# Top-k attention and two expert mixtures on one core: where the work ahead of a branch ends

## Chip, cores and metric

One core of a Trainium2 chip runs the whole program in one launch. The metric is the device time of an execution in microseconds (us). The engines are TensorE (PE; its weight loads are PEld), VectorE (DVE), ScalarE (ACT), GpSimd (POOL) and SyncE (SP, which here only issues transfers).

## The reference

```python
def _attn_ref(q, k, v):                      # (2, 8, 576, 64): batch, heads, tokens, width
    scores = q @ k.T / 8                     # per batch and head
    keep the 32 largest of each row, softmax over them, times v
    ...
def _moe_ref(x, domain_probs, w1, w2):       # x 1152 x 512; 4 experts, w1 512 x 1024, w2 1024 x 512
    out += p[:, e:e + 1] * (np.maximum(x @ w1[e], 0.0) @ w2[e])      # every token, every expert
    ...
def _moe2_ref(x, w_gate, w1, w2, capacity):  # 8 experts, capacity 288
    expert_idx = np.argmax(x @ w_gate, axis=1)
    # each token goes to its one expert, at most 288 of them, in order of tokens
    out[i] = gate_w[i] * y[expert_idx[i], pos[i]]
```

How many tokens an expert of the second mixture has is known only on the chip.

## The kernel before

**Order.** The program is written engine by engine by a planner that runs while the kernel is built (class `Order`). Each kind of work is a stream, a Python generator (`w_loads`, `w_splits`, `m1`, `hid`, `htr`, `m2`, `outs`, `gathers`, `prep_x` and others), that yields its next step: the engines that could do it with their costs, the events it waits for, and the buffers (`Slots`) it takes. `run` picks the step with the smallest key: its planned start plus the bias of its stream. For a step on TensorE the key is at least the time when the step is ready plus a slack by stream. `self.now` is the planned start of the last step picked, `busy` the planned end of each engine's last step. Where a step has two engines, the second must win by the penalty `pen`, 1.0 us in the stage of the change. The planned times decide the order alone: on the chip each engine runs its own list in order, and waits for semaphores of the others.

**Weights.** A quarter of an expert is a pair of tiles of 128 x 1024 (part 0 for the first product, part 1 for the second), 512 KB each. `w_loads` issues a load on SP (L341) into one of nine raw tiles. `w_splits` makes a high part in the reduced format on ScalarE (L353) and the low part, raw minus high, on GpSimd or VectorE (L355), which frees the raw tile. There are seven high and seven low tiles for each part: four quarters of the running expert, and three of the next. Products are three matrix multiplications (high x high, high x low, low x high).

**The second mixture.** Tokens are routed, and expert `e` has up to three units of 128 tokens (`b` = 0, 1, 2). A unit is: gather its rows of x (POOL, L1071), transpose them (`prep_x`, PE L1083, ACT L1087, DVE L1090), first product per quarter (`m1`, PE L697), ReLU (ACT L719), transpose (`htr`, PE L755), hidden tile's high and low part (ACT L762, DVE L765), second product (`m2`, PE L794), scaled output (ACT L1102), scatter (POOL, L1106). Unit 0 is always run. Units 1 and 2 stand in the bodies of branches (`more`, L1142) on the count of tokens, which is loaded at L1163 on every engine. Within a body only the unit's own streams run: `more` sets the other streams aside and restores the plan behind the body, whether it will run or not. The next expert's unit 0 comes behind the branch. The planner counts a body as taking no time.

Ahead of the branch the loop runs the planner until a list of things has been placed:

```python
        nxt = []
        if e + 1 < E2:
            nxt += [("w", NQ1 + 4 * e + 4 + i, part) for i in range(NXTQ) for part in range(2)]
            nxt += [("xgl", e + 1, 0)] if AHEAD else []
        nxt += [("xgl", e, 1), ("xg", e, 2)]
        o.run(until=lambda: all(x in ev for x in nxt))
```

`("w", j, part)` is a quarter's split, `("xgl", e, b)` the transposed input of a unit, `("xg", e, 2)` a gather. The running expert's four quarters are freed behind the branch.

Of the kernel before, what the change touches and what calls it, by code (L numbers as in the profile page):

```python
# [11 lines left out]
AF = mybir.ActivationFunctionType  # L12
# [18 lines left out]
COLD = 12  # L31
BIAS2 = {"w_splits": 0.5}
AHEAD = 1
BATCH = 4
DRATE = 290e3
SLACK = {"transposes": 1.0, "avs": 0.6, "routes": 2.0, "m1": 0.3, "m2": 0.3, "qks": 0.2}
NXTQ = 3
INF = float("inf")
BELOW = 2.0 ** 80
# [27 lines left out]
class Order:  # L67
# [25 lines left out]
    def run(self, until=None):  # L93
        while self.streams and (until is None or not until()):
            pick = None
            for s in self.streams:
                engs, deps, slots = s[2]
                r = 0.0
                for d in deps:
                    r = max(r, s[4] if d == "<" else self.ev.get(d, INF))  # L100
                if r == INF:
                    continue
                for q in set(slots):
                    r = max(r, sorted(q.free)[slots.count(q) - 1] if slots.count(q) <= len(q.free) else INF)
                if r == INF:
                    continue
                opt = None
                for e, c in engs:
                    c *= 2 if e == "PE" and self.now < COLD else 1
                    st = max(r, self.busy.get(e, 0.0))  # L110
                    pen = 0.0 if opt is None else self.pen
                    if opt is None or st + c + pen < opt[0]:
                        opt = (st + c + pen, st, e, c)
                key = opt[1] + s[0]
                if opt[2] == "PE":
                    key = max(key, r + SLACK.get(s[3], 0.0) + s[0])
                if pick is None or key < pick[0]:
                    pick = (key, s, opt)
            if pick is None:
                raise RuntimeError("no stream can go on: " + str([(s[3], s[2][1]) for s in self.streams]))  # L120
            _, s, (_, st, e, c) = pick
            got = []
            for q in s[2][2]:
                i = q.best()[1]
                q.free[i] = INF
                got.append(i)
            self.now = st
            self.busy[e] = st + c
            s[4] = st + c + self.LAT
            self.step(s, (st + c, e, got))  # L130

    pen = 0.0
    bias = {}

    def rebias(self, bias):
# [4 lines left out]
    def set(self, name, t, lat=None):  # L140
        self.ev[name] = t + (self.LAT if lat is None else lat)
# [10 lines left out]
def c_act(n, ps=False, extra=0):  # L152
    return (n / 1.2 + (55 if ps else 95) + 93 * extra) / 1000


def c_dve(n):
    return (n + 64) / 960
# [11 lines left out]
def kernel(  # L169
# [14 lines left out]
    nc = tc.nc  # L184
# [6 lines left out]
    E2 = moe2_w1.shape[0]  # L191
# [25 lines left out]
    o = Order()  # L217
    ev = o.ev
# [4 lines left out]
    def slots(pool, n, shape, dt, name):  # L223
        return Slots(tiles(pool, n, shape, dt, name))
# [6 lines left out]
    def act(c, deps=(), sl=()):  # L231
        return [("ACT", c)], deps, sl
# [7 lines left out]
    def sub(n, deps=(), sl=()):  # L240
        return [("POOL", c_pool(n)), ("DVE", c_dve(n))], deps, sl

    def eng_of(e):
        return {"POOL": nc.gpsimd, "DVE": nc.vector}[e]
# [71 lines left out]
    NQ1 = len(GROUPS) * E1 * 4  # L316
# [4 lines left out]
    w_lo = [slots(wp, 3, WSH[i], F32R, f"w{i}l") for i in range(2)]  # L321
    w_hi = [slots(wp, 3, WSH[i], F32R, f"w{i}h") for i in range(2)]
# [24 lines left out]
    def w_splits():  # L347
        for j in range(NQF, NQ):
            for part in range(2):
                t, _, (i, l) = yield act(c_act(1024), [("wr", j, part)], [w_hi[part], w_lo[part]])  # L350
                raw, r = W[j, part]
                hi, lo = w_hi[part].tiles[i], w_lo[part].tiles[l]
                nc.scalar.activation(hi, raw, AF.Copy)  # L353
                t, e, _ = yield sub(1024, ["<"])
                eng_of(e).tensor_sub(lo, raw, hi.bitcast(F32))  # L355
                w_raw.free[r] = t
                W[j, part] = [lo, l, hi, i]
                o.set(("w", j, part), t)

    def w_free(j, part, t):  # L360
        if j < NQF:
            w_raw.free[W.pop((j, part))[1]] = t
            return
        _, l, _, h = W.pop((j, part))
        w_lo[part].free[l] = t
        w_hi[part].free[h] = t
# [484 lines left out]
    def logits(tl):  # L851
        n = len(tl)
        t0 = tl[0]
        _, _, (pl_i,) = yield pe(0.01, [("acc", t0)], [banks])
        pl = banks.tiles[pl_i]
        xts = []
        for t in tl:
            _, _, (g, xi) = yield pe(4 * 0.112, [("acc", t)], [banks, xt_s])
            xts.append(xi)
            a = acc_s.tiles[acc[t]]  # L860
            px, xt = banks.tiles[g], xt_s.tiles[xi]
            nc.sync.dma_start(x1[t * P:(t + 1) * P, :], a)
            for c in range(ND):
                nc.tensor.transpose(px[:, c * P:(c + 1) * P], a[:, c * P:(c + 1) * P], ident)
            tm, e, _ = yield [("ACT", c_act(512, True)), ("DVE", c_dve(512))], ["<"], []
            if e == "ACT":
                nc.scalar.activation(xt, px, AF.Copy)
            else:
                nc.vector.tensor_copy(xt, px)
            banks.free[g] = tm  # L870
            acc_s.free[acc[t]] = tm + 3.0
            o.set(("xt", t), tm)
        for i, t in enumerate(tl):
            xt = xt_s.tiles[xts[i]]
            tm, _, _ = yield pe(0.35, [("xt", t)])
            for c in range(ND):
                nc.tensor.matmul(pl[:, i * E2:(i + 1) * E2], xt[:, c, :], wg[:, c, :],
                                 start=(c == 0), stop=(c == ND - 1))
            xt_s.free[xts[i]] = tm
            o.set(("lg", t), tm)  # L880
        if tl[-1] == NT - 1:
            return pl_i
        tm, _, _ = yield dve(0.12, [("lg", tl[-1])])
        nc.vector.tensor_copy(LG[:, t0:t0 + n].rearrange("p n e -> p (n e)"), pl[:, :n * E2])
        banks.free[pl_i] = tm
        for t in tl:
            o.set(("lg", t), tm)
# [121 lines left out]
    def routes():  # L1009
# [3 lines left out]
        early = range(GROUPS[-1][0])  # L1013
        for i in range(0, len(early), BATCH):
            yield from route(early[i:i + BATCH], late_pool[0])
        pl_i = yield from logits(GROUPS[-1])
# [98 lines left out]
    def unit(e, b):  # L1115
        class Lazy:
            def __init__(self, n):
                self.n = n

            def __getitem__(self, key):  # L1120
                return XG[e, b][self.n][key]
        J = Job(("u", e, b), Lazy(0), Lazy(1), 1, [NQ1 + e * 4 + i for i in range(4)], [("xg_ok", e, b)],
                unit_out(e, b), False, True)
        return [o.add(m1([J]), "m1"), o.add(hid([J]), "hid"), o.add(htr([J]), "htr"),
                o.add(m2([J]), "m2"), o.add(outs([J]), "outs")]

    def finish(ss):
        o.run(until=lambda: not any(s in o.streams for s in ss))

    order = [(e, b) for e in range(E2) for b in range(UB)]  # L1130
    ph_s.extend(range(2), o.now)
    o.rebias(BIAS2)
# [6 lines left out]
    def more(e, b):  # L1139
        if b == UB:  # L1140
            return
        with tc.If(n > b * P):  # L1142
            st = o.save()
            o.streams = []
            ss = []
            if b > 1:
                ss.append(o.add(prep_x([(e, b)]), "prep_x"))
            ss += unit(e, b)
            finish(ss)
            more(e, b + 1)  # L1150
            o.restore(st)

    for e in range(E2):
        ev["go", e] = o.busy["PE"]
        finish(unit(e, 0))
        nxt = []
        if e + 1 < E2:
            nxt += [("w", NQ1 + 4 * e + 4 + i, part) for i in range(NXTQ) for part in range(2)]
            nxt += [("xgl", e + 1, 0)] if AHEAD else []
        nxt += [("xgl", e, 1), ("xg", e, 2)]  # L1160
        o.run(until=lambda: all(x in ev for x in nxt))
        o.run(until=lambda: "gates" in ev)
        n = nc.values_load(cnt[0:1, e:e + 1], min_val=0, max_val=NTOK)  # L1163
        more(e, 1)
        XG_s.free[XG[e, 1][2]] = o.busy["PE"]
        for b in range(2, UB):
            xg_s.free[xgs[e, b]] = o.busy["PE"]
        for i in range(4):
            for part in range(2):
                w_free(NQ1 + 4 * e + i, part, o.busy["PE"])  # L1170
# [35 lines left out]
```

## Time and profile before

| what | value |
|---|---|
| three runs, median | 849.49 us (848.1 to 850.31) |
| the profiled execution | 851.02 us, of which 849.0 us are the span from first to last instruction |
| TensorE busy | 777.7 us, 92% of the span |
| VectorE, ScalarE, GpSimd busy | 630.4, 592.2, 419.5 us |
| mean granted TensorE clock | 0.969 of full |
| second mixture | from about 656 us to the end; twelve units (L1106 has 12 scatters) |

By the trace the units of experts 0 to 7 are 2, 1, 2, 3, 1, 1, 1 and 1. In the rows below times are us from the span's start; a row of time order is start, length, engine, line, operation, output<-inputs, count, and in brackets the idle time before it with what ended it.

### The profile page before, as it was taken

The numbers are of one execution on the slowest core, as the hardware profiler recorded it, in microseconds if no ns is written. First come the engines' busy times: TensorE is split into PE (matmuls) and PEld (weight loads), VectorE is DVE, ScalarE is ACT, GpSimd is POOL, SyncE is SP. The second block draws the span as 40 slices with busy tenths as digits, with TensorE's granted clock in tenths as the row PEclk, the third lists the DMA queues.
The fourth block names the chain that finished last, engine by engine and source line by source line (L and its number), as shares of the span: only waits on it lengthen the run. The fifth ranks groups of instructions, "written<-read, shape, count | busy, mean of one in ns | idle before, by whom it ended". The sixth has DMA issues, their size and how long they took to land. (4 is left out here: it accounts for less than half of the span.)

```text
span 849.0 us, 15682 instructions
## 1 busy us (share of the span) xinstructions
PE 777.7 (92%) x5538; PEld 685.4 (81%) x5538; DVE 630.4 (74%) x1475; ACT 592.2 (70%) x1199; POOL 419.5 (49%) x292
## 2 busy tenths in 40 slices
PE   6668999899999999999999999999995989997676
PEld 5557777699889989899988898998983979887665
DVE  6799999999999998999998386568445266515551
ACT  6767878888999988989888765445442356626552
POOL 4332233766779977789985612222333143403321
PEclk9999999899999999999999999999996999999889
DMA  5344865722345543335552698555566159617630
GB/s 139 112 119 118 248 204 184 227 98 96 92 132 170 159 141 119 125 122 177 174 159 85 216 367 286 180 173 171 182 195 207 42 192 311 209 63 223 215 107 10
DMA packets 116953, 138.96 MB, mean 164 GB/s; under 512 B 18911, under 2 KB 84959, under 8 KB 116864
## 3 DMA queue, kind: packets, MB, share of 16 engines
q1 hardware_dynamic: 113712, 129.23, 47.7%
q0 software_dynamic: 2880, 8.52, 3.2%
q8 instruction: 51, 0.84, 0.4%
q14 instruction: 38, 0.31, 0.1%
q10 hardware_dynamic: 272, 0.07, 0.0%
HBM read 130.84 MB, written 7.86 MB: 163 GB/s over the span
## 5 line engine op out<-in xcount | busy, mean ns | idle before, releaser
L554 DVE MAX8 m<-wk 128x8 f32<-128x576 f32 x216 | 158.6, 749 | 0.8
L572 POOL TENSOR_TENSOR e<-sc,e 128x576 f32<-128x576 f32 x72 | 102.5, 1426 | 74.6 <-ACT e L570 66.7
L355 POOL TENSOR_TENSOR w0l<-wraw,w0h 128x1024 fp32r<-128x1024 f32 x42 | 101.3, 2411 | 27.7 <-ACT w0h L353 21.7
L550 DVE MATCH_REPLACE8 wk<-m,wk 128x576 f32<-128x576 f32 x144 | 106.9, 743 | 0.0
L355 POOL TENSOR_TENSOR w1l<-wraw,w1h 128x1024 fp32r<-128x1024 f32 x39 | 93.9, 2408 | 18.8 <-ACT w1h L353 17.9
L737 ACT ACTIVATE hh<-bank 128x256 fp32r<-128x256 f32 x128 | 49.8, 390 | 75.8 <-PE bank L794 65.1
L794 PE MATMUL bank<-w1h,hh 128*128 128x512 f32 x220 | 91.3, 415 | 1.0 <-ACT hh L762 1.0
L794 PE MATMUL bank<-w1h,hl 128*128 128x512 f32 x220 | 86.5, 393 | 0.1
L794 PE MATMUL bank<-w1l,hh 128*128 128x512 f32 x220 | 86.5, 393 | 0.0
L740 DVE SCALAR_TENSOR_TENSOR hl<-bank,hh 128x256 fp32r<-128x256 f32 x128 | 53.6, 420 | 42.3 <-ACT hh L737 41.5
L700 PE MATMUL bank<-xh,w0h 128*128 128x256 f32 x392 | 66.6, 293 | 0.0
L605 PE MATMUL bank<-ident,e 128*128 128x128 f32 x288 | 47.5, 291 | 20.6 <-ACT e L593 20.6
L520 PE MATMUL bank<-kT,qT 128*128 128x288 f32 x320 | 64.2, 333 | 0.7 <-ACT qT L498 0.6
L700 PE MATMUL bank<-xh,w0l 128*128 128x256 f32 x392 | 63.2, 284 | 0.0
L700 PE MATMUL bank<-xl,w0h 128*128 128x256 f32 x392 | 63.0, 283 | 0.0
L581 ACT ACTIVATE e<-e,m 128x576 f32<-128x576 f32 x72 | 56.3, 781 | 9.3 <-POOL e L572 8.6
L570 ACT ACTIVATE e<-sc,m 128x576 f32<-128x576 f32 x72 | 56.3, 783 | 7.3 <-DVE m L557 6.9
L605 PEld LDWEIGHTS bank<-ident,e 128*128 128x128 f32 x288 | 36.0, 148 | 30.8 <-ACT e L593 22.7
L700 PEld LDWEIGHTS bank<-xh,w0h 128*128 128x128 f32 x392 | 55.7, 191 | 4.0 <-issue 1.4
L593 ACT ACTIVATE e<-e,sm 128x576 f32<-128x576 f32 x72 | 56.0, 782 | 4.0 <-DVE sm L590 3.9
L520 PEld LDWEIGHTS bank<-kT,qT 128*128 128x128 f32 x320 | 51.1, 206 | 8.0 <-issue 4.8
L353 ACT ACTIVATE w1h<-wraw 128x1024 fp32r<-128x1024 f32 x52 | 55.8, 1072 | 1.7 <-PE bank L794 1.7
(199 smaller groups left out, 2070.1 us busy)
## 6 DMA issues: line engine op xcount, KB each, us to landing
wraw<-in_moe_w_dram SPq DMA_DIRECT2D x160, 512.0 KB, 3.8
wrawb<-in_moe_w_dram SPq DMA_DIRECT2D x64, 512.0 KB, 4.7
out_dram<-zero SPq DMA_DIRECT2D x9, 256.0 KB, 3.6
x<-acc SPq DMA_DIRECT2D x9, 256.0 KB, 4.2
kr<-in_k_dram SPq DMA_DIRECT2D x8, 256.0 KB, 2.7
vt<-in_v_dram SPq DMA_DIRECT2D x8, 256.0 KB, 3.5
qr<-in_q_dram SPq DMA_DIRECT2D x31, 64.0 KB, 2.3
acc<-x,gidx POOLq DMA_INDIRECT x24, 4.5
```

What stands on the lines that cost most here:

```text
L353: nc.scalar.activation(hi, raw, AF.Copy)
L355: eng_of(e).tensor_sub(lo, raw, hi.bitcast(F32))
L520: nc.tensor.matmul(banks.tiles[g[y]][:, :HS], qT_s.tiles[i][:, 2 * a + m % 2], kT_s.tiles[kT[b, 2 * pr + a]][:, half * HS:(half + 1) * HS] ...
L550: nc.vector.match_replace(wk, m[:, 8 * r - 8:8 * r], s if r == 1 else wk, -3.0e38)
L554: nc.vector.max(m[:, 8 * r:8 * r + 8], wk)
L570: nc.scalar.activation(e, s, AF.Relu, bias=m[:, TOPK:TOPK + 1], scale=-BELOW)
L572: nc.gpsimd.tensor_sub(e, s, e)
L581: nc.scalar.activation(e, e, AF.Exp, bias=m[:, TOPK + 1:TOPK + 2], accum_out=sm_s[a].tiles[i][:, 0:1])
L593: nc.scalar.activation(e, e, AF.Copy, scale=s[:, 1:2])
L605: nc.tensor.transpose(x[:, n * P:(n + 1) * P], p[:, a, a * REST + n * P:a * REST + (n + 1) * P], ident)
L700: nc.tensor.matmul(ph[:, :N], w[:, c, fc * P:(fc + 1) * P], xx[:, c, :N], start=(c == 0 and m == 0), stop=(c == ND - 1 and m == 2))
L794: nc.tensor.matmul(y, hx[:, col:col + P], w[:, fc, :], start=(first and m == 0), stop=(qi == 3 and fc == 1 and m == 2))
```

## The change

Four things change, all in the planner.

- The work ahead of a branch must include only the first quarter of the next expert (both parts), the transposed input of this expert's second unit, and the gather for the third. The rest of the former list is still run for only until a picked step starts later than 0.8 us (`MEET`) ahead of the planned end of TensorE's unit.
- Then `push("w_loads")` runs the loads alone until no raw tile is left to give out.
- In the second mixture's quarters (`j >= NQ1`) the high part may go to ScalarE or VectorE.
- In the second mixture `w_splits` is in `late`: its key, too, is at least the ready time plus a slack, of 0.6 us.

```diff
+MEET = 0.8
...
-SLACK = {"transposes": 1.0, "avs": 0.6, "routes": 2.0, "m1": 0.3, "m2": 0.3, "qks": 0.2}
+SLACK = {"transposes": 1.0, "avs": 0.6, "routes": 2.0, "m1": 0.3, "m2": 0.3, "qks": 0.2, "w_splits": 0.6}
...
                 key = opt[1] + s[0]
-                if opt[2] == "PE":
+                if opt[2] == "PE" or s[3] in self.late:
                     key = max(key, r + SLACK.get(s[3], 0.0) + s[0])
...
+    def push(self, name):
+        kept = self.streams
+        self.streams = [s for s in kept if s[3] == name]
+        gone = list(self.streams)
+        try:
+            self.run()
+        except RuntimeError:
+            pass
+        self.streams = [s for s in kept if s not in gone or s in self.streams]
...
+    late = ()
...
-                t, _, (i, l) = yield act(c_act(1024), [("wr", j, part)], [w_hi[part], w_lo[part]])
+                who = [("ACT", c_act(1024))] + [("DVE", c_dve(1024))] * (j >= NQ1)
+                t, e, (i, l) = yield who, [("wr", j, part)], [w_hi[part], w_lo[part]]
                 raw, r = W[j, part]
                 hi, lo = w_hi[part].tiles[i], w_lo[part].tiles[l]
-                nc.scalar.activation(hi, raw, AF.Copy)
+                if e == "ACT":
+                    nc.scalar.activation(hi, raw, AF.Copy)
+                else:
+                    nc.vector.tensor_copy(hi, raw)
...
+    o.late = ("w_splits",)
...
-        nxt += [("xgl", e, 1), ("xg", e, 2)]
-        o.run(until=lambda: all(x in ev for x in nxt))
+        must = [("xgl", e, 1), ("xg", e, 2)] + nxt[:2 if e + 1 < E2 else 0]
+        end = o.busy["PE"] - MEET
+        o.run(until=lambda: all(x in ev for x in must) and (o.now > end or all(x in ev for x in nxt)))
+        o.push("w_loads")
         o.run(until=lambda: "gates" in ev)
```

## Rows read from the trace of the kernel before

**Rows 1.** The page: TensorE's busy time; the granted clock by slices.
```profile
PE 777.7 (92%) x5538; PEld 685.4 (81%) x5538; DVE 630.4 (74%) x1475; ACT 592.2 (70%) x1199; POOL 419.5 (49%) x292
...
PEclk9999999899999999999999999999996999999889
```

**Rows 2.** Stages: length, busy PE, PEld, DVE, ACT, POOL (x instructions), clock, DMA, GB/s.
```profile
684.00:700.00 16.00, 13.54 (x91) 12.12 (x92) 12.58 (x13) 12.12 (x20) 9.01 (x6) 1.00 0.75 250
700.00:726.00 26.00, 25.22 (x168) 22.65 (x166) 14.22 (x17) 15.44 (x28) 7.49 (x6) 1.00 0.78 257
...
765.00:782.60 17.60, 13.34 (x91) 11.88 (x89) 12.29 (x14) 12.61 (x20) 7.27 (x6) 1.00 0.74 226
782.60:804.40 21.80, 15.20 (x89) 13.40 (x89) 11.99 (x13) 12.07 (x19) 7.57 (x6) 0.83 0.63 208
804.40:827.00 22.60, 16.62 (x88) 14.19 (x89) 11.39 (x13) 12.19 (x19) 4.82 (x3) 0.80 0.40 135
827.00:849.00 22.00, 15.27 (x84) 12.89 (x84) 3.80 (x6) 6.03 (x12) 3.42 (x2) 0.89 0.03 10
```

**Rows 3.** TensorE in order of time: what follows the branches of experts 1 to 6.
```profile
699.73 0.63 PE L1083 MATMUL bank<-ident,acc 128*128 128x128 f32 x4 [2.11 <-DVEq L1142]
...
712.84 0.65 PE L697 MATMUL bank<-w0h,xh 128*128 128x256 f32 x4
...
726.04 0.66 PE L1083 MATMUL bank<-ident,acc 128*128 128x128 f32 x4 [0.82 <-ACTq L1142]
...
782.59 0.71 PE L697 MATMUL bank<-w0hb,xh 128*128 128x256 f32 x4 [4.26 <-DVEq L1142]
...
804.38 1.19 PE L697 MATMUL bank<-w0h,xh 128*128 128x256 f32 x4 [6.53 <-DVEq L1142]
...
827.02 1.19 PE L697 MATMUL bank<-w0hb,xh 128*128 128x256 f32 x4 [5.43 <-DVEq L1142]
```

**Rows 4.** VectorE in order of time: low parts ahead of branches 1, 2, 4, 6.
```profile
696.76 2.82 DVE L355 TENSOR_TENSOR w1lb<-wraw,w1hb 128x1024 fp32r<-128x1024 f32 x1 [0.51 <-ACT w1hb L353]
...
712.11 2.67 DVE L355 TENSOR_TENSOR w1lb<-wraw,w1hb 128x1024 fp32r<-128x1024 f32 x1 [0.67 <-ACT w1hb L353]
...
780.03 1.23 DVE L355 TENSOR_TENSOR w0lb<-wrawb,w0hb 128x1024 fp32r<-128x1024 f32 x1 [1.43 <-ACT w0hb L353]
781.17 1.22 DVE L355 TENSOR_TENSOR w1lb<-wrawb,w1hb 128x1024 fp32r<-128x1024 f32 x1
...
825.60 1.22 DVE L355 TENSOR_TENSOR w1lb<-wrawb,w1hb 128x1024 fp32r<-128x1024 f32 x1
```

**Rows 5.** ScalarE in order of time: high parts (L353) and scaled outputs (L1102).
```profile
695.68 1.04 ACT L353 ACTIVATE w1hb<-wraw 128x1024 fp32r<-128x1024 f32 x1
...
725.26 0.69 ACT L1102 ACTIVATE x1T<-bank,gate 128x512 f32<-128x512 f32 x1 [4.50 <-PE bank L794]
...
778.37 0.69 ACT L1102 ACTIVATE x1T<-bank,gate 128x512 f32<-128x512 f32 x1 [1.21 <-PE bank L794]
778.95 1.05 ACT L353 ACTIVATE w0hb<-wrawb 128x1024 fp32r<-128x1024 f32 x1
779.90 1.04 ACT L353 ACTIVATE w1hb<-wrawb 128x1024 fp32r<-128x1024 f32 x1
...
801.31 1.04 ACT L353 ACTIVATE w1hb<-wrawb 128x1024 fp32r<-128x1024 f32 x1
...
824.13 1.05 ACT L353 ACTIVATE w1hb<-wrawb 128x1024 fp32r<-128x1024 f32 x1
```

**Rows 6.** TensorE in order of time: two first-product quarters; expert 7's input transposed.
```profile
765.13 0.63 PE L697 MATMUL bank<-w0h,xh 128*128 128x256 f32 x4
...
766.91 0.72 PE L697 MATMUL bank<-w0h,xh 128*128 128x256 f32 x4
...
815.75 0.60 PE L1083 MATMUL bank<-ident,acc 128*128 128x128 f32 x4
```

**Rows 7.** SP in order of time: raw loads issued around expert 3's second and third units.
```profile
741.59 27.03 SPq L341 DMA_DIRECT2D wraw<-in_moe_w_dram  x2
```

## The prediction, made before the changed kernel was run

> **What bounds the kernel now.** The page comes first. TensorE is busy 92% of the span, and its granted clock is full in all but the first slices and the last ones [rows 1]. Up to about 640 us nothing the change touches can therefore bring much; what is to be had lies where that row falls, in the second mixture.
>
> The second view is the table by stages, cut at the experts' first units [rows 2]. Of the twelve units that ran, experts 0 and 2 have two, expert 3 has three, and 1, 4, 5, 6 and 7 have one. An expert with one unit costs TensorE 13.3 us (684 to 700: 13.54 busy, 765 to 782.6: 13.34). But the stretches of experts 4, 5 and 6 last 17.6, 21.8 and 22.6 us, and in the last two the clock is 0.83 and 0.80. ScalarE is busy 12.1 to 12.6 us in each, VectorE 11.4 to 12.3. No engine is full, so something makes them take turns.
>
> TensorE's order of time shows what [rows 3]. It stands still 2.10 us before 699.73, 4.26 before 782.59, 6.53 before 804.38 and 5.43 before 827.02, 18.3 us in all, each time released by VectorE's passing of the branch (L1142). These are the branches of experts 1, 4, 5 and 6, whose second unit does not run. At expert 2's branch, where it does run, TensorE goes on at 712.84 with no idle time. After a second unit it waits 0.82 us for ScalarE.
>
> VectorE's and ScalarE's orders of time say what is late [rows 4, 5]. VectorE's last low part ahead of expert 1's branch ends at 696.76 + 2.82 = 699.58, expert 4's at 781.17 + 1.22 = 782.39, expert 6's at 825.60 + 1.22 = 826.82; TensorE starts 0.15 to 0.20 us later in all of the four. So its first matmul of the next expert waits until VectorE has worked off everything that the program put ahead of the branch. Much of that was begun after TensorE had finished: its unit of expert 4 ended at 782.59 - 4.26 = 778.33, and two high parts start on ScalarE at 778.95 and 779.90, behind the scaled output of 778.37; expert 5 has four such (the last at 801.31), expert 6 three (the last at 824.13), nine together. They belong to the second and third quarter of the next expert, which TensorE needs only some microseconds into its next unit. That is the bound: three quarters are demanded ahead of the branch, and the branch makes TensorE wait for them.
>
> **The change, part by part.** *Where the work ahead of the branch ends.* What remains ahead of it is what the planner starts before TensorE's unit ends, the next first quarter, and the second unit's input. ScalarE's scaled output is still there: 0.69 us from 725.26, ended 0.09 before TensorE's 726.04 [rows 3, 5]. So 0.83 us is the floor of a gap. The ceiling is a low part begun just at the unit's end: with 1.23 us plus the 0.20 it gives 1.43. I take 1.1, nearer to the floor because ScalarE's output comes first in any case: four gaps of 18.3 us become 4.4. Gain 13.9 (12.6 to 15.0).
>
> *The clock.* The gap of 2.10 us left the clock at 1.00 (700 to 726); those of 4.26, 6.53 and 5.43 are followed by stretches at 0.83, 0.80 and 0.89, between the levels of 1.2 and 2.4 GHz [rows 2]. TensorE's busy time in these is 15.20, 16.62 and 15.27 us for 89, 88 and 84 matmuls, against 13.34 for 91: 1.9 + 3.3 + 1.9 = 7.1 us more. Gaps of 1.1 us are shorter than the one that did no harm, so I take 6 back (0 if the gaps stay over 4 us).
>
> *The nine high parts and their low parts* move behind the branch, into the next unit, and here is the cost. From a high part's start to its low part's end is 778.95 to 780.03 + 1.23 = 781.26, that is 2.93 us behind the unit's end; two low parts follow each other by 1.14, so a quarter (two splits) takes 2.3 us. TensorE takes its first-product quarters 766.91 - 765.13 = 1.78 apart, a transposing group between them included [rows 6]. With the one guaranteed quarter in hand, TensorE starts 0.83 behind the unit's end and wants the second quarter at 2.6, gets it at 2.9 (wait 0.3); wants the third at 4.7, gets it at 5.2 (0.5); the fourth at 7.0, gets it at 7.5 (0.5). That is 1.3 us in a unit; with two quarters in hand nothing. Expert 4's branch has two done already (only two high parts start behind its unit's end), so expert 5 pays nothing; experts 6 and 7 pay 1.3 each, 2.6. The same two engines must also serve the unit's own hidden tiles, which go first; for that I double it, to 5 us. Bounds: nothing (12.1 us of ScalarE in 14 us leave room), and nine splits with no cover at VectorE's pace, 9 x 1.14 = 10.3.
>
> *The slack of 0.6 us* lets a split be placed behind another engine step due within that time. It can leave VectorE or ScalarE idle up to 0.6 per split, 4.8 for an expert's eight; nothing if the step it yields to releases TensorE. It is held inside the bounds just given, as both engines have about 2 us to spare per unit.
>
> *High parts on VectorE.* The choice costs a microsecond of penalty, so it is taken only where ScalarE's planned queue is over a microsecond behind. The trace has no such copy; the nearest row is the subtraction of the same size, 1.23 us [rows 4], against about 0.95 between high parts on ScalarE [rows 5]. Few will move, VectorE carries as much as ScalarE, and I put it at nothing (plus or minus 1 us for four of them). The Trainium skill (VectorE: DVE Perf Modes, The perf-mode tier table) has a single-source fp32 copy at twice the rate of a two-source operation, 1227 ns for 2048 elements; halved, that would be some 0.6 us as an estimate and would make four of them worth 2 us less VectorE time, the path being the same. No run here shows it.
>
> *Raw loads given out.* SP has only these loads in this stage, so nothing is queued behind them. The merged row at 741.59 [rows 7] stretches over 27.03 us for two issues: one load stood until expert 3's third unit was over. Given out ahead it lands sooner, but no split in the second mixture is shown waiting for a load, so this is worth nothing, in either direction, unless the splits run ahead of the loads.
>
> *The next expert's input* is no longer demanded ahead of the branch. Its transposes stand well within the unit (815.75 for expert 7, while expert 6's unit ends at 827.02 - 5.43 = 821.59 [rows 3, 6]). If they slipped behind the branch, each would cost its 0.6 us of transposes and about the 0.83 floor again, 1.4, 4.2 for three. I take nothing.
>
> Sum: -13.9 - 6 + 5 = -14.9 us. The profiled execution took 851.02 us (span 849.00), 1.53 above the median; it would take 836.1, and the median 849.49 becomes **834.6**. With every term at its good end (-15.0 - 7.1) it is 827.4; at its bad end (-12.6 - 6 + 10.3) 841.
>
> **A rule that speaks against it.** At the four branches TensorE starts within 0.20 us of the end of VectorE's last low part, and at 712.84 it enters a body with no gap [rows 3, 4]. The Trainium skill (Runtime: NRT & Kernel Launch, Instruction fetch mechanics) says that a taken branch whose target lies outside the fetched pages stalls until the target's page has come. By that rule the gaps would belong to the branch, moving work would not shorten them, and the sum would be nothing in place of -14.9; the rows agree with it badly.
>
> **The rivals.**
>
> *Everything is covered.* The two engines' 12 us per expert fit into 14; then no split is waited for: 827 to 828. Against it: each unit's own tiles cut into the splitting.
>
> *The wait moves into the units.* Splits and unit share two queues in program order. If the four units 4 to 7 stay paced by the splits, 15 of the 19.9 us come back as short waits in the middle of the units, and the clock alone is won: 844.5. For it: ScalarE makes the hidden tiles of the unit between the splits, and each of those waits for TensorE, so a split behind one starts late even where its load has long landed. Against it: in expert 1 all eight high parts were done (the last from 695.68) before the unit's end at 697.63 [rows 3, 5].
>
> *The gap is the branch's own.* If jumping over a body that does not run is what costs the 2.1 to 6.5 us, on whichever engine, the four gaps of 18.3 us and the slow clock behind them stay: 849.5. For it: the long gaps come only where a second unit's body is jumped over. Against it: the 0.15 to 0.20 us behind VectorE's last low part at all four, and the 0.82 us behind expert 2's second unit, where the third unit's body is jumped over too [rows 3, 4].
>
> *Slower: the stock shrinks.* A quarter not split before a second unit isn't split during it either. The units of experts 2 to 7 would then start with one quarter instead of three. It decides at 19.9 / 6 = 3.3 us of waiting per unit, which is where TensorE takes the quarters one by one (a quarter 2.3 us late twice); at 4 us per unit the time is 849.5 + 24 - 19.9 = 853.6. Against it: expert 1 again; in experts 1 to 3 little is left to defer.
>
> **How the numbers follow.** Forecast (829 to 841) 0.50; everything covered 0.14; wait moves into the units 0.18; branch's own 0.08; slower 0.10. Range 826 to 846: it holds the first three, 0.82. A change under 0.3% (2.5 us) can't be told from none by a measurement of this kernel. Faster by more: 0.82; within: 0.08; slower: 0.10.
>
> **What would show it.** Right: the idle time before the first matmul of experts 2, 5, 6 and 7 is 0.8 to 1.5 us, released by ScalarE or VectorE at the branch; clock about 1.00 from 765 on; new waits for low parts (L355 or its successor) inside the units of experts 6 and 7, 5 us together; stretches of experts 4, 5 and 6 of 14 to 16 us. Wrong: gaps unchanged though VectorE is through earlier; waits over 3 us in each first unit; TensorE waiting at units' starts for an input transposed behind the branch; splits waiting for raw loads.

## The result, and the profile after

The changed kernel takes 841.74 us (five runs, 840.96 to 842.24), the kernel before 849.82 (five runs, 848.1 to 850.63): a ratio of 0.9901 with a 95% interval of 0.9881 to 0.9921. It is faster by 8.1 us; 834.6 had been forecast, in a range of 826 to 846. The profiled executions are 842.1 and 851.02 us, their spans 840.3 and 849.0.

The page after, TensorE's busy time and the granted clock by slices:

```profile
PE 776.2 (92%) x5538; PEld 680.7 (81%) x5538; DVE 629.7 (75%) x1465; ACT 592.1 (70%) x1198; POOL 447.3 (53%) x303
...
PEclk9869999899999999999999999999997898999998
```

VectorE and ScalarE have as much work as before [rows 1]; GpSimd has 28 us more. The stages after, cut at the first units of experts 1, 2, 4, 5, 6 and 7 (columns as in [rows 2]):

```profile
681.47:698.34 16.87, 13.32 (x88) 11.76 (x89) 12.14 (x12) 11.09 (x18) 14.62 (x9) 0.96 0.68 215
698.34:727.16 28.82, 28.00 (x168) 25.41 (x168) 13.52 (x15) 15.52 (x28) 12.46 (x7) 0.90 0.74 245
...
766.30:781.31 15.01, 13.43 (x89) 11.68 (x88) 8.64 (x9) 10.61 (x18) 10.42 (x7) 1.00 0.53 163
781.31:797.92 16.61, 14.47 (x89) 11.56 (x89) 10.71 (x11) 10.42 (x17) 9.03 (x6) 1.00 0.88 279
797.92:815.82 17.90, 14.64 (x89) 11.68 (x89) 10.88 (x11) 13.34 (x20) 11.83 (x7) 1.00 0.81 248
815.82:840.30 24.48, 15.95 (x84) 12.46 (x84) 9.40 (x10) 9.05 (x16) 4.08 (x3) 0.86 0.04 14
```

TensorE after, in order of time, where the branches of experts 1, 2, 4, 5 and 6 lie behind it:

```profile
698.34 1.09 PE L1100 MATMUL bank<-ident,acc 128*128 128x128 f32 x4 [3.55 <-DVEq L1160]
...
713.98 0.63 PE L714 MATMUL bank<-w0h,xh 128*128 128x256 f32 x4
...
781.31 0.71 PE L714 MATMUL bank<-w0hb,xh 128*128 128x256 f32 x4 [1.47 <-DVEq L1160]
...
797.92 0.74 PE L714 MATMUL bank<-w0h,xh 128*128 128x256 f32 x4 [0.82 <-ACTq L1160]
...
815.82 0.71 PE L714 MATMUL bank<-w0hb,xh 128*128 128x256 f32 x4 [1.75 <-DVEq L1160]
```

Against [rows 3] three gaps shrank, from 4.26, 6.53 and 5.43 us to 1.47, 0.82 and 1.75. The first of the four grew, from 2.11 to 3.55, and behind it the clock fell to 0.90, where it had been 1.00 [rows 2]. The same view inside expert 6's unit shows new, short waits:

```profile
800.15 0.44 PE L772 MATMUL bank<-ident,hs 128*128 128x128 f32 x2 [0.53 <-ACT hs L736]
...
803.54 0.75 PE L714 MATMUL bank<-w0l,xh 128*128 128x256 f32 x4 [0.32 <-POOL w0l L372]
...
805.29 0.44 PE L772 MATMUL bank<-ident,hs 128*128 128x128 f32 x2 [0.53 <-ACT hs L736]
```

Why the gap behind expert 1 grew is read from VectorE's and GpSimd's orders of time, ahead of that branch:

```profile
691.30 2.42 DVE L372 TENSOR_TENSOR w0l<-wrawb,w0h 128x1024 fp32r<-128x1024 f32 x1
693.65 3.40 DVE L372 TENSOR_TENSOR w0lb<-wrawb,w0hb 128x1024 fp32r<-128x1024 f32 x1
696.97 1.21 DVE L372 TENSOR_TENSOR w1lb<-wraw,w1hb 128x1024 fp32r<-128x1024 f32 x1
```

```profile
690.23 2.42 POOL L372 TENSOR_TENSOR w1l<-wrawb,w1h 128x1024 fp32r<-128x1024 f32 x1
692.58 3.38 POOL L372 TENSOR_TENSOR w1lb<-wraw,w1hb 128x1024 fp32r<-128x1024 f32 x1
```

Low parts now stand close together at the unit's end, on both engines at once. On VectorE one takes 2.42 and 3.40 us beside GpSimd's, and 1.21 alone; GpSimd's own goes from 2.4 to 3.4. The ends of these rows show how: VectorE's two end 1.07 and 1.09 us behind the one on GpSimd that each overlaps (693.72 behind 692.65, 697.05 behind 695.96), and GpSimd's of 692.58 ends 2.24 us behind VectorE's of 691.30. The two engines take turns on these subtractions. In the kernel before the unit had one low part on GpSimd, now it has three.

From the two profiles, by stretches:

| stretch | before | after | difference |
|---|---|---|---|
| start to expert 1's unit | 684.36 | 681.47 | -2.9 |
| four gaps (experts 1, 4, 5, 6) | 18.3 | 7.6 | -10.7 |
| units of experts 5, 6, 7 (15.3, 17.2, 15.9; 15.8, 16.1, 18.4) | 48.3 | 50.3 | +2.0 |
| expert 2's two units with the wait behind them | 26.3 | 28.8 | +2.5 |
| the rest | | | +0.4 |

Up to expert 1's unit all five engines have the same instructions in the same order in both kernels, so the first row is not the change; in the profiles of this study that point lies anywhere from 680.0 to 684.4. The change itself is worth some 6 us between these profiles, 8.1 between the medians, and the rest of that difference stays open.

### The profile page after: what moved, and what is told of

Its sections match the earlier page's. It is cut to its first block, busy times and chain, and to the rows that moved or that the text cites. A ratio compares the mean times of both kernels' runs of the same rounds, so it can differ in the third digit from the quotient of the medians.

```text
span 840.3 us, 15681 instructions
## 1 busy us (share of the span) xinstructions
PE 776.2 (92%) x5538; PEld 680.7 (81%) x5538; DVE 629.7 (75%) x1465; ACT 592.1 (70%) x1198; POOL 447.3 (53%) x303
## 5 line engine op out<-in xcount | busy, mean ns | idle before, releaser
L372 POOL TENSOR_TENSOR w0l<-wraw,w0h 128x1024 fp32r<-128x1024 f32 x44 | 106.1, 2411 | 27.4 <-ACT w0h L368 21.4
L372 POOL TENSOR_TENSOR w1l<-wraw,w1h 128x1024 fp32r<-128x1024 f32 x44 | 107.0, 2431 | 24.4 <-ACT w1h L368 23.3
L811 PE MATMUL bank<-w1h,hh 128*128 128x512 f32 x220 | 91.3, 415 | 0.0
L811 PE MATMUL bank<-w1l,hh 128*128 128x512 f32 x220 | 86.4, 393 | 0.0
L811 PE MATMUL bank<-w1h,hl 128*128 128x512 f32 x220 | 86.2, 392 | 0.0
```

Of the source, the lines that this page charges most:

```text
L811: nc.tensor.matmul(y, hx[:, col:col + P], w[:, fc, :], start=(first and m == 0), stop=(qi == 3 and fc == 1 and m == 2))
```

## The experiments

All are timed in five rounds beside the kernel before, which had 849.4 to 850.0 us.

**The slack taken out** (837.25 us, ratio 0.9851, 0.9827 to 0.9876).

```diff
-    o.late = ("w_splits",)
+    o.late = ()
```

> The changed kernel with w_splits taken out of the late streams, so that splits have no slack of 0.6 us; the cut of the work ahead of a branch, the choice of engine for the high parts and the loads given out stay. Theory A (the slack starts the splits late in a unit, so that the low parts bunch at its end): the gap behind expert 1 falls from 3.54 to at most 2.1 us, expert 2 runs at full clock (2.5 us less), the units of experts 5 to 7 wait less; about 837 us against 841.7. Theory B (the low parts that the plan gave to GpSimd stretch those on VectorE, whatever the slack): the gap stays over 3 us where low parts still run on both engines; 841 to 842. Theory C (the order inside the units of experts 5 to 7 follows the planned arrival of the loads): the gap behind expert 1 shrinks, but units 5 to 7 still last 15.8 to 18.2 us.

The gap behind expert 1 is 1.95 us, and its unit has one low part on GpSimd again; the last low part on VectorE still takes 2.65 us. The units of experts 5 to 7 last 13.4, 16.3 and 17.6 us, the last two partly at a slow clock (0.91 and 0.90). So the slack costs 4.5 us; theory A holds for expert 1, theory B is not refuted (the one stretched low part is the gap), theory C is alive in experts 6 and 7. Expert 2's full clock did not come: behind 1.95 us its stretch is at 0.94.

**High parts on ScalarE alone** (845.96 us, 0.9956, 0.9934 to 0.9977).

```diff
-                who = [("ACT", c_act(1024))] + [("DVE", c_dve(1024))] * (j >= NQ1)
+                who = [("ACT", c_act(1024))]
```

> The changed kernel with all high parts on ScalarE again; one high part moves back from VectorE. Theory A: the same within 2 us of 841.7, since the slack stays. Rival: the one copy on VectorE, ahead of expert 1's input on that engine, is what set expert 1 back; then the gap behind expert 1 is again about 2.1 us and the time about 838.

Neither came true: 4.2 us slower than the changed kernel, though a single high part moves back. The order of all that follows it changes too; the last experiment takes this up.

**The cut alone** (836.28 us, 0.9837, 0.9809 to 0.9865).

```diff
-        nxt += [("xgl", e, 1), ("xg", e, 2)]
-        o.run(until=lambda: all(x in ev for x in nxt))
+        must = [("xgl", e, 1), ("xg", e, 2)] + nxt[:2 if e + 1 < E2 else 0]
+        end = o.busy["PE"] - MEET
+        o.run(until=lambda: all(x in ev for x in must) and (o.now > end or all(x in ev for x in nxt)))
```

> The kernel before with only the cut of the work ahead of a branch: no slack, no choice of engine for high parts, no loads given out. Theory A: as the kernel without slack, about 837 us, the gaps behind experts 4 to 6 at 0.8 to 1.8 us. If the choice of engine or the slack carries the gain instead: 846 or more.

The cut carries the whole gain, and more than the change brought. Of the other parts, the loads given out (`push`) do nothing at all: without it the changed kernel's program is the same, instruction for instruction, on every engine.

**Slack and choice of engine without the cut** (853.1 us, 1.003, 1.0009 to 1.005).

```diff
-        o.run(until=lambda: all(x in ev for x in must) and (o.now > end or all(x in ev for x in nxt)))
+        o.run(until=lambda: all(x in ev for x in must) and all(x in ev for x in nxt))
```

> The changed kernel with the whole former list demanded ahead of each branch (three quarters and the next input), so slack and choice of engine alone. If the cut carries the gain: the gaps behind experts 4 to 6 are back at 4 to 7 us, and by theory A that behind expert 1 is 3.5 us or more, so 850 to 855 us. If slack or choice of engine carries it: below 846.

As theory A has it. TensorE in order of time, behind the branches of experts 4, 5 and 6:

```profile
785.03 1.19 PE L714 MATMUL bank<-w0hb,xh 128*128 128x256 f32 x4 [4.49 <-DVEq L1160]
...
807.83 1.19 PE L714 MATMUL bank<-w0h,xh 128*128 128x256 f32 x4 [6.54 <-DVEq L1160]
...
829.60 1.19 PE L714 MATMUL bank<-w0hb,xh 128*128 128x256 f32 x4 [6.54 <-DVEq L1160]
```

**One part fewer demanded ahead** (on the cut alone; 834.75 us, 0.9835, 0.9814 to 0.9856).

```diff
-        must = [("xgl", e, 1), ("xg", e, 2)] + nxt[:2 if e + 1 < E2 else 0]
+        must = [("xgl", e, 1), ("xg", e, 2)] + nxt[:1 if e + 1 < E2 else 0]
```

> The kernel with the cut alone, and of the next first quarter only the part for the first product is demanded ahead of the branch. By the orders one pair of instructions moves: at expert 6's branch the last high part on ScalarE and its low part on VectorE go behind it. If what remains of the gaps is work demanded ahead that TensorE does not need yet: expert 6's gap falls from 3.13 to about 0.9 us and the time from 836.3 by 2 us, to 834. Rival: the part is missed later, in the second product of expert 7, and the time stays within 1 us of 836.3.

TensorE behind expert 6's branch, first with the cut alone, then with the part moved:

```profile
812.05 0.71 PE L714 MATMUL bank<-w0hb,xh 128*128 128x256 f32 x4 [3.13 <-DVEq L1160]
```

```profile
809.51 0.71 PE L714 MATMUL bank<-w0hb,xh 128*128 128x256 f32 x4 [0.90 <-ACTq L1160]
```

The gap does as expected, and expert 7's unit is no longer for it (17.25 us in both). The medians differ by 1.5 us, which the intervals cannot separate from none; the rows can.

**A faster transfer rate in the plan** (on the cut alone; 832.73 us, 0.9802, 0.9777 to 0.9827).

```diff
+    rate = [DRATE]
...
-        o.dma = max(o.dma, t) + nbytes / DRATE
+        o.dma = max(o.dma, t) + nbytes / rate[0]
...
     o.rebias(BIAS2)
+    rate[0] = 600e3
```

> The kernel with the cut alone, the planner's transfer rate raised from 290 to 600 GB/s from the second mixture on, so that the plan no longer expects loads to come late. Theory C (the units of experts 5 to 7 lose time because their order follows loads planned later than they land): units of 6 and 7 fall from 15.1 and 17.3 us to under 14, ahead of each branch more is split, gaps grow a little; 830 to 833 us. Rival (the units are paced by ScalarE and VectorE themselves): units and time unchanged, 835 to 838. Rival (TensorE then waits for loads that have not landed): slower than 838.

No wait over 0.3 us is left inside the units of experts 5 to 7, and none is for a load. They last 14.8, 14.8 and 14.3 us, part of it at a slow clock behind gaps of 1.9 us:

```profile
777.85:794.58 16.73, 14.82 (x88) 13.38 (x89) 12.68 (x13) 12.14 (x19) 6.96 (x6) 0.90 0.96 318
794.58:811.30 16.72, 14.80 (x88) 13.38 (x89) 12.64 (x13) 12.14 (x19) 6.94 (x5) 0.90 0.46 154
```

The order has changed. TensorE inside expert 7's unit, with the cut alone: the second product (L811) comes between first-product quarters (L714), behind two waits for a hidden tile.

```profile
814.25 0.44 PE L772 MATMUL bank<-ident,hs 128*128 128x128 f32 x2 [0.53 <-ACT hs L736]
...
815.47 0.50 PE L811 MATMUL bank<-w1h,hh 128*128 128x512 f32 x1 [0.34 <-ACT hh L779]
...
816.97 0.63 PE L714 MATMUL bank<-w0hb,xh 128*128 128x256 f32 x4
```

At 600 GB/s the last first-product quarter (L716) stands ahead of the first second product (L813), with no wait:

```profile
817.93 0.72 PE L716 MATMUL bank<-w0h,xh 128*128 128x256 f32 x4
...
819.58 0.48 PE L813 MATMUL bank<-w1h,hh 128*128 128x512 f32 x1
```

So theory C holds for the waits: at 290 GB/s the plan falls behind (an expert's eight loads of 512 KB take 14.5 us at that rate, its unit 13.3 us of TensorE), has TensorE do a quarter's second product before it starts the next quarter's first, and on the chip, where the loads have landed, that order leaves the hidden tile's way through ScalarE and VectorE uncovered. Its forecast of units under 14 us did not come true, as TensorE's busy time is longer at the slow clock. At 600 GB/s the cut has nothing left to cut: the kernel before with this rate and without the cut gives the same program, instruction for instruction.

**Low parts on VectorE alone**, from the eighth quarter of the second mixture on (on the cut alone; 836.85 us, 0.9842, 0.9815 to 0.9869).

```diff
-                t, e, _ = yield sub(1024, ["<"])
+                t, e, _ = yield dve(c_dve(1024), ["<"]) if j >= NQ1 + 7 else sub(1024, ["<"])
```

> The kernel with the cut alone, and all low parts of the second mixture's ahead work on VectorE, none on GpSimd. Theory B (low parts side by side on GpSimd and VectorE stretch each other): VectorE's rows of 1.9 to 2.8 us become 1.23, the gaps behind experts 1 and 5 fall from 1.95 and 1.85 to about 1 us, 1 to 2 us faster, 834.5 to 835.5. Rival: VectorE has 9.8 us of low parts per expert instead of some 8 and becomes late; 838 or more.

Half a miss: the gap behind expert 1 fell from 1.95 to 0.90 us, but expert 5's stayed (1.83), the units of experts 6 and 7 grew by 1.4 and 0.7 us, and the time is unchanged. Expert 5's gap was never a stretched low part: the second low part of the demanded quarter starts on VectorE at 790.72, 0.40 us behind the unit's end, and takes 1.22. The growth of the two units is the clock, 0.91 in both, where the cut alone has 1.00: TensorE is busy 15.3 and 15.8 us there in place of 14.1 and 14.7, and idle about as long. So the unchanged time does not show that the choice of engine is worth nothing here.

**The same on the changed kernel** (835.31 us, 0.9835, 0.9808 to 0.9863).

```diff
-                t, e, _ = yield sub(1024, ["<"])
+                t, e, _ = yield dve(c_dve(1024), ["<"]) if j >= NQ1 + 7 else sub(1024, ["<"])
```

> The changed kernel, slack and all, with all low parts of the second mixture's ahead work on VectorE. If the slack does its harm through the low parts that it sends to GpSimd: the gap behind expert 1 falls from 3.54 to under 2 us, expert 2 keeps the full clock, about 838 us. If it does it by starting the splits late, whichever engine takes them: the gap stays about 3 us or more, 841 us or slower.

The changed kernel loses 6.4 us by its low parts on GpSimd, and the slack does its harm there through them: with all low parts on VectorE the time with the slack and the choice of engine is 835.31 us, without both 836.85 (the run before this), where with GpSimd it was 841.74 and 836.28. VectorE ahead of expert 1's branch, slack and all:

```profile
692.35 1.22 DVE L372 TENSOR_TENSOR w1lb<-wraw,w1hb 128x1024 fp32r<-128x1024 f32 x1
693.49 1.22 DVE L372 TENSOR_TENSOR w0lb<-wrawb,w0hb 128x1024 fp32r<-128x1024 f32 x1
694.62 1.22 DVE L372 TENSOR_TENSOR w1lb<-wraw,w1hb 128x1024 fp32r<-128x1024 f32 x1
```

They follow each other by 1.13 us where they took 2.4 and 3.4, and TensorE waits 1.37 us at that branch.

**Cut, planned rate and low parts on VectorE together** (on the cut alone; 825.3 us, 0.9709, 0.9689 to 0.9728).

```diff
-                t, e, _ = yield sub(1024, ["<"])
+                t, e, _ = yield dve(c_dve(1024), ["<"]) if j >= NQ1 + 7 else sub(1024, ["<"])
...
     o.rebias(BIAS2)
+    rate[0] = 600e3
```

> The kernel with the cut, the planner's transfer rate of 600 GB/s and all low parts of the second mixture's ahead work on VectorE. If the gaps of 1.92 us left at 600 GB/s are low parts stretched beside GpSimd's, and the slow clock behind them (0.85 to 0.94) comes with their length: gaps of 0.9 to 1.2 us at the branches of experts 1, 4, 5 and 6, clock near 1.00, 826 to 829 us. Rival: VectorE, then busy for 13 us in a unit, ends later than it did with GpSimd's help, gaps of 2 us or more, 832 us or slower.

It beats both kernels, by 24.2 and 16.4 us. TensorE behind the branches of experts 1 and 4 to 6, and the stages of experts 4 to 6:

```profile
694.21 0.63 PE L1102 MATMUL bank<-ident,acc 128*128 128x128 f32 x4 [0.89 <-DVEq L1163]
...
774.27 0.63 PE L1102 MATMUL bank<-ident,acc 128*128 128x128 f32 x4 [0.87 <-ACTq L1163]
...
788.40 0.63 PE L1102 MATMUL bank<-ident,acc 128*128 128x128 f32 x4 [0.86 <-ACTq L1163]
...
802.52 0.63 PE L1102 MATMUL bank<-ident,acc 128*128 128x128 f32 x4 [0.87 <-ACTq L1163]
```

```profile
760.52:774.27 13.75, 12.88 (x85) 11.46 (x85) 12.26 (x14) 11.99 (x19) 6.20 (x4) 1.00 0.71 227
774.27:788.40 14.13, 13.28 (x88) 11.84 (x89) 12.18 (x14) 12.05 (x19) 4.56 (x4) 1.00 1.05 352
788.40:802.52 14.12, 13.25 (x88) 11.83 (x89) 12.16 (x14) 12.04 (x19) 4.43 (x3) 1.00 0.69 238
```

An expert takes 14.1 us, 13.3 of TensorE and the 0.87 of ScalarE's scaled output, with both other engines busy 12 us under it and the transfers at 352 GB/s in one stage, waited for by nobody. Here, too, the cut moves nothing: without it the program is the same, instruction for instruction. The planned rate and the low parts on VectorE carry this gain.

**The slack doubled** (845.17 us, 0.9941, 0.9922 to 0.9961).

```diff
-SLACK = {"transposes": 1.0, "avs": 0.6, "routes": 2.0, "m1": 0.3, "m2": 0.3, "qks": 0.2, "w_splits": 0.6}
+SLACK = {"transposes": 1.0, "avs": 0.6, "routes": 2.0, "m1": 0.3, "m2": 0.3, "qks": 0.2, "w_splits": 1.2}
```

> The changed kernel with a slack of 1.2 us for the splits in place of 0.6. If the slack is what costs the changed kernel its 4 to 5 us: more low parts bunched at the ends of the units, gap behind expert 1 of 3.5 us or more, units of experts 5 to 7 longer still, 844 us or slower. If the loss comes from the one particular order that 0.6 gives: anything between 836 and 842.

The time follows the slack, 837.25 at none, 841.74 at 0.6 and 845.17 at 1.2, but not by the place expected: the gap behind expert 1 is 1.92 us, the other three 0.8 to 0.9, and TensorE waits 1.0 to 1.2 us for a low part in the middle of each of the units of experts 4 to 7:

```profile
780.49 0.74 PE L714 MATMUL bank<-w0l,xh 128*128 128x256 f32 x4 [1.06 <-DVE w0l L372]
```

**The slack in the fastest kernel** (834.3 us, 0.9797, 0.9773 to 0.9821).

```diff
-    o.late = ()
+    o.late = ("w_splits",)
```

> The fastest kernel so far (cut, planned rate of 600 GB/s, low parts on VectorE; 825.3 us) with the slack of 0.6 us for splits put back. If the slack does harm only through low parts on GpSimd and through loads that are planned late, both gone here: 824 to 827 us. If starting the splits late costs by itself: new waits for low parts in the units of experts 5 to 7 and gaps over 1 us, 828 us or slower.

9 us slower, with no low part on GpSimd and no load planned late: starting the splits late costs by itself. The gaps behind experts 1, 4, 5 and 6 are 1.16 to 1.35 us, and in experts 3 to 6 there is a wait of 0.78 us for a hidden tile behind high parts on ScalarE. From expert 5's first matmul to expert 6's it takes 16.07 us in place of 14.13.

**High parts on ScalarE, low parts on VectorE, with slack** (834.84 us, 0.9811, 0.9791 to 0.983).

```diff
-                who = [("ACT", c_act(1024))] + [("DVE", c_dve(1024))] * (j >= NQ1)
+                who = [("ACT", c_act(1024))]
...
-                t, e, _ = yield sub(1024, ["<"])
+                t, e, _ = yield dve(c_dve(1024), ["<"]) if j >= NQ1 + 7 else sub(1024, ["<"])
```

> The changed kernel with all high parts on ScalarE (845.96 us) and all low parts of the second mixture's ahead work on VectorE. If that kernel's 4 us over the changed one come from its low parts on GpSimd: about 836 us, as the changed kernel with low parts on VectorE (835.3). If the one high part on VectorE is worth something of its own under the slack: 838 us or slower.

So the 4.2 us that the one high part on VectorE seemed to be worth were GpSimd's low parts again, which another order placed worse.

## Why the prediction was right in direction, and off in size

*The mechanism was right, and half of it was missing.* TensorE's waits at the branches ended with VectorE's work put ahead of them, and the cut took most of them away. Without the cut the gaps behind experts 4 to 6 are 4.5 to 6.5 us again. The branch's own cost, the third rival, is at most the 0.82 to 0.90 us left in the fastest kernel. In the fourteen profiles every gap that ends with the passing of a branch does so 0.15 to 0.21 us behind the last instruction of VectorE, or 0.09 to 0.19 us behind the last one of ScalarE, whichever released it. The rule on fetching the target's page, in the Trainium skill (Runtime: NRT & Kernel Launch, Instruction fetch mechanics), would put the cost in the jump; the gaps followed the work ahead of the jump in every run. Of the last 0.82 us ScalarE's scaled output is 0.69, and no run tells whether part of the rest is such a fetch. What the prediction lacked is why the work came so late. It named the three quarters demanded as the bound; at 600 GB/s the kernel that demands the same three quarters has gaps of 1.91 to 1.95 us behind experts 1, 4, 5 and 6, and of 0.86 to 0.89 with the low parts on VectorE. The demand cost as much as it did because the plan expected the loads late.

*The gaps* were forecast at 4.4 us and are 7.6. The step that failed is the ceiling of 1.43 us, a low part begun at the unit's end. Of the 3.2 us too much, 2.4 are the gap behind expert 1 (3.55 in place of 1.1). A low part beside one on GpSimd takes 3.40 us ahead of that branch, though the 2.82 us row of before already stood in [rows 4]; and the second part of the demanded quarter, which the sum did not price, holds TensorE by itself (in the cut alone 3.13 us, 0.90 when it went).

*The slack of 0.6 us* got no term in the sum, because VectorE and ScalarE had two microseconds to spare per unit. That step failed most plainly: 4.5 us here, by low parts bunched at the unit's end on two engines at once, and 9 us in the fastest kernel, by waits for the hidden tile and longer gaps. With the slow planned rate and the low parts on VectorE it costs nothing that could be measured, so its price depends on the order that it falls into. Spare time in a stage is no cover when the work is started late within it and the branch asks for the end.

*The waits inside the units* were put at 5 us, for low parts, in experts 6 and 7. The fastest kernel's units of experts 5 to 7 last 13.3, 13.3 and 12.8 us, 39.4 together, so the changed kernel's 50.3 are 10.9 us longer. Of these, 5.2 us are idle time of TensorE (1.2 in the kernel before), most of it in waits of 0.3 to 0.8 us for hidden tiles on ScalarE, with one of 0.32 for a low part. The rest is longer busy time, part of it at a slow clock in expert 7's unit; the trace does not show how much of it is waiting between matmuls. The prediction had the cause wrong too: not splits that come too late for TensorE, but an order made for loads that the plan expected too late, and the slack on top of it. The rival "everything is covered" (827 to 828) is what happens when order and low parts are put right, at 825.3; the rival of waits moved into the units (844.5) is what the changed kernel partly does, and 841.74 lies nearer to it than to the forecast of 834.6. The time is at the sum's own bad end (841).

*The clock.* The slow stretches of experts 5 and 6 are gone (1.00), as forecast. Expert 7's is not (0.86, before 0.89): it moved from the unit's start to the middle. And one came behind expert 1's longer gap (0.90, 2.5 us). That a gap of 2.11 us did no harm was read from one execution; at 1.9 to 1.95 us other kernels show 0.90, 0.94 and 1.00, and behind 3.13 us the cut alone shows 1.00, the kernel without slack 0.90. The prediction also read the clock's row wrongly, without consequence: it falls to 6 in the slice from 637 to 658 us too (0.65), where both kernels have the same program, and a 9 in it means 0.9 or more.

*High parts on VectorE:* one was moved. It took 0.69 us, near the 0.6 estimated from the Trainium skill (VectorE: DVE Perf Modes, The perf-mode tier table) and not the 1.23 of the nearest row; it is worth nothing by itself. *Raw loads given out:* worth nothing, as forecast. *The next input* caused no wait at a branch in the changed kernel.

## What to carry to other kernels

Work ahead of a branch that is not done when the engine gets there is paid in full where the body is passed over, so either it is placed early enough to be done, or only what the other side needs first belongs there. Where a planner orders the work, look first at whether its costs agree with the trace: here one constant, a transfer rate under what the loads did on the chip, made the late order that the cut then repaired, and correcting it gave the same program with or without the cut. A delay rule that yields to other work should be tested at zero and at double before it is kept.

## What the runs showed of the hardware that was not expected

Two low parts of 128 x 1024 at once on VectorE and GpSimd take turns. In the second mixture, in the profiles of the kernel before and of the changed one, a low part on VectorE that begins beside one on GpSimd ends 1.07 to 1.15 us behind it (1.22 us alone, up to 3.42 so), and one on GpSimd that begins beside VectorE's ends 2.24 to 2.28 us behind that (2.40 alone, up to 3.42 so). VectorE's subtraction from `bank` for the hidden tile (L782) keeps its 0.42 us beside GpSimd's low part. The Trainium skill (GPSIMD Engine Reference, Specifications) has the two share their SBUF interfaces when VectorE reads two inputs there, which agrees. A pair side by side costs some 3.3 us (1.08 + 2.24, an estimate), where VectorE alone does two in 2.3.

The granted clock fell behind some idle stretches of 1.9 us (0.94 and 0.90 at the planned rate of 600 GB/s) and not behind others of the same length (1.00 behind 1.95 us in the cut alone). It also fell where no single wait was that long: in the changed kernel TensorE is busy 0.44 us of the 1.40 from 825.00 to 826.40, in two waits of 0.47 and 0.78 us, and the clock from 826.40 to 829.00 is 0.58.
